# A prelude in a written order: the inverse's chain first, the first softmax in two halves of tokens

## The chip, the cores and the metric

The kernel runs on one core of a Trainium2 chip. The metric is the device time of one execution in microseconds (us); lower is better. TensorE does matrix products, VectorE, ScalarE and GpSimd work element by element, and SyncE issues the DMAs. In the profile they are PE (PEld for its weight loads), DVE, ACT, POOL and SP.

## The reference

Three stages follow one another: a Nystrom attention, a gated feed-forward layer and a soft mixture of experts. Cut to what matters (8 batches, 8 heads, 576 tokens, head size 64, 32 landmarks):

```python
q_lm, k_lm = means of q, k over 18 tokens each          # landmarks
A  = softmax(q @ k_lm.T / 8)                            # 576 x 32
Bm = softmax(q_lm @ k_lm.T / 8)                         # 32 x 32
C  = softmax(q_lm @ k.T / 8)                            # 32 x 576
Z  = Bm.T / (norm_1(Bm) * norm_inf(Bm) + 1e-6)
for _ in range(6): Z = 2 * Z - Z @ Bm @ Z               # inverse
x  = A @ Z @ C @ v                                      # attention
x  = (silu(x @ w_gate) * (x @ w_val)) @ w_out           # 512 -> 1536 -> 512
logits = x @ phi                                        # soft mixture of 8 experts
out = softmax(logits) @ experts(softmax(logits, tokens).T @ x)
```

All is float32. The feed-forward weights arrive as 64-bit floats (w_cat: gate and value of one slice of 128 columns side by side; w_out) and are converted on the chip.

## The kernel before

The 1536 feed-forward columns are cut into 12 slices (j), the 576 tokens into two halves of 288. A unit (b, j) computes both halves of slice j for batch b: `mm3` (line 885) takes six products each for pg and pv out of A's softmax, split into a high and a low part (EH, EL), and of g = Z C v times the weights, split in the same way (GH by line 728, GL by line 742). ScalarE applies silu to pg (u, line 302), VectorE multiplies u by pv (hT, line 914) and transposes hT (line 762). Batch b+1's attention runs in between, cut into steps that lists of numbers place in the slots of the units, four slots a unit.

Batch 0 has nothing before it, so a prelude does its attention: `first_attention`. Landmark sums over q and k (line 323), scores for A, B and C (lines 530 and 366), the softmax of B, from it the start value R of an inverse (line 468), five rounds that square R (line 457) and multiply T by it (lines 478 to 481), in between C's softmax, its transposes (line 397) and its product with v (line 407). Then VD (line 515), the small matrix WB (line 524), and g of unit 0. A's softmax of batch 0 comes from the generator `a_softmax` over all 576 tokens: maximum (line 683), subtraction on GpSimd (684), exponent, sum (675), reciprocal, product on GpSimd (687), transpose (681), EH on ScalarE (689), EL on GpSimd (690).

A weight tile is converted by one Prelu on ScalarE (line 166), shifts on VectorE (line 182) and an or on VectorE (line 183), the last two once per 512 columns. A w tile has 1024 columns, a w_out tile 512. w_out tiles are then transposed and multiplied by phi (lines 259 to 275).

What is written sets no order here: a scheduler orders each engine's instructions by its own estimates, within the dependencies. Each engine runs its queue in that order. `SCHED` holds the places: `w` and `o` say in which slot a conversion begins, where a negative number means the prelude, `p` places w_out's further steps, `loads` is the order of the first DMAs behind q, k and the constants, `side` a string of steps that are mixed into the prelude. w0, w1 and w_out's tile 0 belong to the prelude.

Of the kernel before, what the change touches and what calls it, by code (L numbers as in the profile page):

```python
# [8 lines left out]
F32 = mybir.dt.float32  # L9
F32R = mybir.dt.float32r  # L10
# [9 lines left out]
M = 32  # L20
# [33 lines left out]
def nystrom_softmoe_kernel(  # L54
# [15 lines left out]
    pe, act, dve, pool, sp = nc.tensor, nc.scalar, nc.vector, nc.gpsimd, nc.sync  # L70

# [37 lines left out]
    def big(tag, name):  # L109
        return bigp.tile([128, 2048], F32, tag=tag, name=name)  # L110
# [170 lines left out]
    for j in range(NJ):  # L281
        for kind in "wo":
# [8 lines left out]
    side_pre = [f for k in sorted(side_w) if k < 0 for f in side_w[k]]  # L291
# [60 lines left out]
    def first_attention(side):  # L352
        b = 0
        ks, qs, AN, CE = attention_tiles(b)
        NBUF = big("w5", "newton").rearrange("p (i q m) -> p i q m", q=2, m=128)
# [54 lines left out]
        for quad in range(2):  # L410
            for hp in (2 * quad, 2 * quad + 1):
                landmark("k", b, hp, ks)
                landmark("q", b, hp, qs)
            a_scores(quad)
# [11 lines left out]
        for half in range(2):  # L426
            a_nat(0, half)
# [14 lines left out]
        for q in range(2):
            blockdiag(q, nrm[:, q, 0, :], bdB)
        mn = psp.tile([128, 512], F32, tag="l", name="m_nx")
        pe.matmul(mn[:, 0:128], bmask, nrm.rearrange("p q a m -> p (q a m)"), start=True, stop=True)
        side("b")
        for half in range(2):
            a_nat(1, half)
        c_max(0)
        c_exp(0)  # L450
        side("c")
# [9 lines left out]
        ms = squares(bdB)  # L461
        nx = ap.tile([128, 2, 2], F32, tag="nx", name="nx")
# [21 lines left out]
        side("d")  # L484
        mv = psp.tile([128, 512], F32, tag="l", name="m_v")
        for k in range(1, 6):
            ms = squares(R)
            if k > 1:
                T = t_step(T, k - 1)
            R = NBUF[:, k]  # L490
            dve.tensor_copy(R[:, 0, :], ms[0][:, 0:128])
            act.copy(R[:, 1, :], ms[1][:, 0:128])
            if k == 1:
                c_max(1)
                c_exp(1)
# [200 lines left out]


    G_t = {}

    def paired(b, j):  # L700
        return 0 < b < nb - 1 and not (b == nb - 2 and j >= NJ - 2)

    def g_product(b, j, n):

        w = w_t[j // 2].rearrange("p (u h f) -> p u h f", u=2, h=4)
        gs = [psp.tile([128, 512], F32, tag="x", name="g", bufs=3) for r in range(2)]
        for u in range(n):
            assert j + u in w_done
        for hp in range(4):
            for r in range(2):  # L710
                pe.matmul(gs[r][32 * hp:32 * hp + 32, 0:256 * n].rearrange("p (u f) -> p u f", u=n),  # L711
                          WB[b % 2][64 * r:64 * r + 64, hp, :], w[64 * r:64 * r + 64, j % 2:j % 2 + n, hp, :],
                          start=True, stop=True)
        if n == 2:
            side_b = (6 * (b - 1) + j // 2) % 2 == 0
            e, tag = (ap, "b") if side_b else (mp, "")
            parts = [(e.tile([128, 512], F32R, tag="GH" + tag, name="GH", bufs=2),
                      e.tile([128, 512], F32R, tag="GL" + tag, name="GL", bufs=2), gs[r]) for r in range(2)]
        else:
            GH = mp.tile([128, 512], F32R, tag="GH", name="GH", bufs=2)  # L720
            GL = mp.tile([128, 512], F32R, tag="GL", name="GL", bufs=2)
            parts = [(GH[:, 256 * r:256 * r + 256], GL[:, 256 * r:256 * r + 256], gs[r][:, 0:256]) for r in range(2)]
        for r, (H_, L_, g) in enumerate(parts):
            for u in range(n):
                for sel in range(2):
                    c = slice(256 * u + 128 * sel, 256 * u + 128 * sel + 128)
                    G_t[b, j + u, r, sel] = (H_[:, c], L_[:, c])
            act.copy(H_, g)  # L728
            gl_todo.append((L_, g, H_))

    def g_unit(b, j):

        if not paired(b, j):
            g_product(b, j, 1)
        elif j % 2 == 0:
            g_product(b, j, 2)

    gl_todo = []

    def g_low():  # L740
        for GL, g, GH in gl_todo:
            dve.tensor_tensor(out=GL, in0=g, in1=GH, op=ALU.subtract)  # L742
        gl_todo.clear()
# [248 lines left out]
    wo = {}  # L992
# [45 lines left out]
    for b in range(nb):  # L1038
        for j in range(NJ):
# [242 lines left out]
```

## Time and profile before

| | us |
|---|---|
| median of 3 runs | 693.27 (693.15 to 694.85) |
| the profiled execution | 693.29 |
| its span in the trace | 691.5 |

The difference of 1.8 us lies around the span. Busy shares of the span: PE 93%, PEld 69%, DVE 70%, ACT 44%, POOL 10%. These shares are means; the first 122 us, prelude and batch 0, are read by stretches. Times of instructions are counted from the start of the span. The granted clock is a share of 2.4 GHz.

### The profile page before, as it was taken

To read this page: it belongs to the slowest core of one execution; us is meant where nothing else is said; L and a number is where in the kernel's file an instruction comes from. 1 tells how busy PE (TensorE), PEld (TensorE's weight loads), DVE (VectorE), ACT (ScalarE), POOL (GpSimd) and SP (SyncE) were. 2 spreads that over 40 slices of the span, in tenths; PEclk is the share of its full clock that TensorE was granted. 3 is DMA by queue.
4 is the path that set the end of the run, shared out by engine and by line. 5 is a ranking of instruction groups with operands and counts; after the bars stand their busy time and mean duration, and the time that the engine had idled before them with its cause. 6 is when DMAs were issued, how large, how long until landed. Compare 5 with 4: busy or idle time off the path is not lost.

```text
span 691.5 us, 18581 instructions
## 1 busy us (share of the span) xinstructions
PE 646.5 (93%) x7747; PEld 478.0 (69%) x7747; DVE 487.2 (70%) x1189; ACT 306.5 (44%) x775; POOL 72.2 (10%) x81
## 2 busy tenths in 40 slices
PE   5799999999999999999999999999999999999991
PEld 2566667766877787778776877687768876773561
DVE  5999989878667976797579757985786664540341
ACT  2567875356335533463345334533463352321441
POOL 0401012012001200120012001200120000010000
PEclk9899999999999999999999999999999999999997
DMA  8797873142204220322032302230212499599998
GB/s 294 243 361 275 300 263 116 65 138 70 70 2 136 70 72 2 116 78 84 2 101 82 96 1 89 79 110 2 82 50 63 149 301 283 186 295 319 348 371 309
DMA packets 59988, 105.03 MB, mean 152 GB/s; under 512 B 3968, under 2 KB 29696, under 8 KB 58368
## 3 DMA queue, kind: packets, MB, share of 16 engines
q1 hardware_dynamic: 59904, 103.84, 45.8%
q8 instruction: 61, 1.00, 0.6%
q14 instruction: 23, 0.19, 0.1%
HBM read 91.24 MB, written 12.58 MB: 150 GB/s over the span
## 4 chain that ended last, share of the span: by engine, by line
PE 68%; DVE 16%; ACT 7%; issue 3%; DMA 3%; POOL 1%; SPq 0%; ACTq 0%; POOLq 0%; DVEq 0%
PE pg L885 19%; PE pv L885 17%; PE g L711 6%; PE l L757 4%; PE m_n L638 3%; PE m_d L856 3%; PE m_f L1215 2%; PE m_f L1167 2%; DMA q<-in_qT_dram 2%; PE m_a L530 2%; DVE bd L312 2%; ACT L302 2%; DVE GL L742 1%; PE m_o L1198 1%; DVE qs L323 1%
## 5 line engine op out<-in xcount | busy, mean ns | idle before, releaser
L302 ACT ACTIVATE u<-pg 128x288 f32<-128x288 f32 x174 | 71.6, 412 | 148.7 <-PE pg L885 142.9
L914 DVE TENSOR_TENSOR hT<-u,pv 128x288 f32<-128x288 f32 x174 | 78.2, 450 | 56.2 <-PE pv L885 50.3
L885 PE MATMUL pg<-EH,GH 128*128 128x288 f32 x384 | 96.8, 329 | 2.6 <-ACT GH L728 1.6
L885 PE MATMUL pv<-EH,GH 128*128 128x288 f32 x384 | 91.4, 312 | 1.8 <-issue 1.6
L742 DVE TENSOR_TENSOR GL<-g,GH 128x512 fp32r<-128x512 f32 (+1 forms) x122 | 66.4, 569 | 32.6 <-ACT GH L728 32.3
L885 PE MATMUL pg<-EH,GL 128*128 128x288 f32 x384 | 86.0, 299 | 0.0
L885 PE MATMUL pg<-EL,GH 128*128 128x288 f32 x384 | 84.0, 298 | 0.0
L885 PE MATMUL pv<-EH,GL 128*128 128x288 f32 x384 | 83.1, 295 | 0.0
L885 PE MATMUL pv<-EL,GH 128*128 128x288 f32 x384 | 82.7, 296 | 0.0
L728 ACT CAST GH<-g 128x512 fp32r<-128x512 f32 (+1 forms) x122 | 54.3, 497 | 56.3 <-PE g L711 56.2
L885 PEld LDWEIGHTS pg<-EH,GH 128*128 128x128 f32 x384 | 59.9, 189 | 23.6 <-issue 18.9
L885 PEld LDWEIGHTS pv<-EH,GH 128*128 128x128 f32 x384 | 61.5, 188 | 19.6 <-issue 18.0
L762 DVE STREAM_TRANSPOSE HB<-hT 128x576 f32<-128x576 f32 x96 | 73.9, 770 | 1.3
L885 PEld LDWEIGHTS pg<-EH,GL 128*128 128x128 f32 x384 | 62.4, 188 | 2.2 <-issue 2.1
L885 PEld LDWEIGHTS pg<-EL,GH 128*128 128x128 f32 x384 | 61.7, 188 | 1.8 <-issue 1.8
L885 PEld LDWEIGHTS pv<-EH,GL 128*128 128x128 f32 x384 | 61.9, 188 | 0.5 <-issue 0.5
L885 PEld LDWEIGHTS pv<-EL,GH 128*128 128x128 f32 x384 | 61.6, 188 | 0.9 <-issue 0.9
L711 PE MATMUL g<-w,WB 64*32 64x512 f32 (+1 forms) x976 | 56.5, 510 | 0.4 <-ACT WB L524 0.4
L757 PE MATMUL l<-hT,P_sb 128*32 128x128 f32 (+1 forms) x768 | 47.4, 298 | 0.6 <-DVE hT L914 0.6
L757 PEld LDWEIGHTS l<-hT,P_sb 128*32 128x32 f32 x768 | 15.9, 108 | 40.0 <-issue 17.9
L856 PE MATMUL m_d<-HB,HB 32*32 32x384 f32 x1116 | 39.6, 491 | 0.3 <-DVE GL L742 0.3
L684 POOL TENSOR_TENSOR AN<-AN,mxA 128x576 f32<-128x576 f32 x16 | 18.4, 1169 | 181.1 <-DVE mxA L683 165.2
(238 smaller groups left out, 963.2 us busy)
## 6 DMA issues: line engine op xcount, KB each, us to landing
k<-in_kT_dram SPq DMA_DIRECT2D x52, 288.0 KB, 3.9
ffn<-in_w_dram SPq DMA_DIRECT2D x13, 1024.0 KB, 9.4
ffn<-in_w_dram SPq DMA_DIRECT2D x24, 512.0 KB, 8.8
HB<-in_w_cat_dram SPq DMA_DIRECT2D x8, 1024.0 KB, 7.5
v<-in_v_dram SPq DMA_DIRECT2D x8, 1024.0 KB, 5.7
q<-in_qT_dram SPq DMA_DIRECT2D x28, 288.0 KB, 3.2
HB<-in_w_out_dram SPq DMA_DIRECT2D x12, 512.0 KB, 4.9
wr<-in_w_cat_dram SPq DMA_DIRECT2D x4, 1024.0 KB, 8.5
```

What stands on the lines that cost most here:

```text
L302: i = act.activation(*a, **kw)
L312: dve.tensor_tensor(out=dst[:, q, :].rearrange("p (h m) -> p h m", h=4), in0=src.unsqueeze(1).to_broadcast([128, 4, 32]), in1=bm3, op=ALU. ...
L638: pe.matmul(m[:, 96 * q:96 * q + 96], bd[:, q, :], RV[:, q, :], start=True, stop=True)
L684: lambda q: pool.tensor_tensor(out=AN[q], in0=AN[q], in1=bc[q], op=ALU.subtract),
L711: pe.matmul(gs[r][32 * hp:32 * hp + 32, 0:256 * n].rearrange("p (u f) -> p u f", u=n), WB[b % 2][64 * r:64 * r + 64, hp, :], w[64 * r:64 * ...
L728: act.copy(H_, g)
L742: dve.tensor_tensor(out=GL, in0=g, in1=GH, op=ALU.subtract)
L757: pe.matmul(L[32 * c:32 * c + 32, 0:32 * k], P_sb[:, j, :], main[:, 0:k, c, :], start=j == 0, stop=j == NJ - 1)
L762: dve.transpose(HB[b % 2][:, S * j:S * j + S].rearrange("p (t r) -> p t r", r=32), hT[:, 0:S].rearrange("p (t r) -> p t r", r=32))
L856: pe.matmul(ms[a][32 * g:32 * g + 32, 0:384].rearrange("p (j f) -> p j f", j=NJ), d_of(a, g, k), hb[32 * a:32 * a + 32, :, 4 * k + g, :], ...
L885: pe.matmul(ps[:, 0:HALF], G_t[b, j, q, sel_][h], e[:, q, ts_], start=n == 0, stop=n == 5)
L914: dve.tensor_tensor(out=o, in0=u, in1=pv[:, 0:HALF], op=ALU.mult)
```

## The change

The prelude is written as one list, and `keep_order` ties each instruction of PE, ACT and DVE in it to the one before it on the same engine, so that the written order is the queue's order. What belongs to batch 0 is issued behind the last of them on its engine (`after_first`, until batch 1).

In the list the B scores come as soon as the landmarks are there, and B's softmax and the squares before the rest. A's softmax of batch 0 is done in two halves of 288 tokens: the first half between the rounds, the second behind VD, WB, EL of the first half and g of unit 0. Subtraction, product and EL of it are done by DVE, not POOL. Conversions of w0 and w1 stand in the list, w1's with the low words taken off by ACT (`lw`); w_out's tiles 0 and 1 go to slots 1 and 4. The loads come in the order w0, v0, w1, q and k of batch 1, phi, o0, w2, w3, o1, w4, v1.

```diff
 SCHED = {
-    'w': [[-22, 2], [-12, 2], [0, 3], [1, 3], ...
-    'o': [[-6, 1], [3, 2], [5, 3], ...
+    'w': [[0, 0], [0, 0], [0, 3], [2, 3], ...
+    'o': [[1, 2], [4, 2], [5, 3], ...
-    'loads': ['w1', 'q0', 'o0', 'w0', 'v0', 'o1', 'q1', 'v1', 'w2', 'w4', 'p', 'w3'],
+    'loads': ['w0', 'v0', 'w1', 'q0', 'q1', 'p', 'o0', 'w2', 'w3', 'o1', 'w4', 'v1'],
-    'lw': [0, 0, 0, ...
+    'lw': [0, 1, 0, ...
...
+    def keep_order(start):
+        last = {}
+        for i in nc.cur_bb.bb.instructions[start:]:
+            if i.engine in ENGINES:
+                if i.engine in last:
+                    tc.add_manual_dep(i, last[i.engine].name, mybir.DependencyInfo(
+                        mybir.DependencyClass.NoSync, mybir.DependencyReason.DATA), reason="keep_order")
+                last[i.engine] = i
+        return last.values()
...
+        def a_sub(q, h):
+            dve.tensor_tensor(out=AN[q][:, ts_[h], :], in0=AN[q][:, ts_[h], :], in1=bc(q, h), op=ALU.subtract)
+        def a_exp(q, h):
+            in_order("exp", AN[q][:, ts_[h], :], AN[q][:, ts_[h], :], AF.Exp, scale=SC / SEG)
+        def e_low(q, h):
+            dve.tensor_tensor(out=EL[:, q, cs_[h]], in0=AT[q][:, cs_[h]], in1=EH[:, q, cs_[h]], op=ALU.subtract)
...
             if k == 1:
+                both(a_sub, 0)
+                both(a_exp, 0)
+                c_max(0)
+            if k == 2:
+                c_exp(0)
                 c_max(1)
+                both(a_sum, 0)
+            if k == 3:
+                c_t(0)
                 c_exp(1)
+                a_inv(0)
+                both(a_mul, 0)
+            if k == 4:
                 c_t(1)
                 c_v(0, mv)
+                both(a_back, 0)
+            if k == 5:
                 c_v(1, mv)
+                both(e_high, 0)
+                w0[1]()
+                w0[2]()
...
         w_blocks(b, VD, T)
+        both(e_low, 0)
+        g_unit(0, 0)
+        both(a_max, 1)
+        g_low()
+        w1[0]()
+        both(a_sub, 1)
+        both(a_exp, 1)
+        both(a_sum, 1)
+        a_inv(1)
+        both(a_mul, 1)
+        both(a_back, 1)
+        both(e_high, 1)
+        both(e_low, 1)
+        for f in w1[1:]:
+            f()
...
+    start = len(nc.cur_bb.bb.instructions)
+    first_attention()
+    after_first = ctx.enter_context(ExitStack())
+    for i in keep_order(start):
+        after_first.enter_context(tc.issue_after(i))
     load_w(5)
-    for f in side_pre:
-        f()
-    g_unit(0, 0)
-    g_low()
```

VectorE's queue of the kernel before, from VD to the first hT of batch 0 (ks and qs are the landmarks of batch 1, HB_86 holds a w_out tile):

```order
L183 SCALAR_TENSOR_TENSOR HB_86<-HB_86 128x512
L515 TENSOR_SCALAR VD<-m_v_409,rc 128x64 x2
L323 TENSOR_REDUCE ks<-k_0_112 128x32
L323 TENSOR_REDUCE ks<-k_1_116 128x32
L323 TENSOR_REDUCE ks<-qk_124 128x32
L323 TENSOR_REDUCE ks<-qk_127 128x32
L323 TENSOR_REDUCE qs<-q_0_110 128x32
L742 TENSOR_TENSOR GL<-g,GH 128x256 x2
L323 TENSOR_REDUCE qs<-q_1_114 128x32
L323 TENSOR_REDUCE qs<-qk_124 128x32
L323 TENSOR_REDUCE qs<-qk_127 128x32
L914 TENSOR_TENSOR hT<-u,pv 128x288
```

The same queue of the changed kernel, the end of the second half's softmax up to the first hT and the next (w_235 is the tile of w0 and w1, w_462 that of w2 and w3):

```order
L498 STREAM_TRANSPOSE AT<-AN_143 128x288
L504 TENSOR_TENSOR EL<-AT,EH 128x288 x2
L190 SCALAR_TENSOR_TENSOR w_235<-w_235,HB_85 128x512 x2
L334 TENSOR_REDUCE ks<-k_0_116 128x32
L990 TENSOR_TENSOR hT<-u,pv 128x288
L334 TENSOR_REDUCE ks<-k_1_120 128x32
L193 TENSOR_SCALAR w_462<-w_462 128x512 x2
L194 SCALAR_TENSOR_TENSOR w_462<-HB_85,w_462 128x512
L193 TENSOR_SCALAR HB_86<-HB_86 128x512
L407 TENSOR_TENSOR GL<-g,GH 128x256 x2
L194 SCALAR_TENSOR_TENSOR HB_86<-HB_86 128x512
```

Eight landmarks and the w_out tiles stood ahead of the first hT; now one landmark does, and the others and the w_out tiles stand among the products of the first units, while a half of the softmax has come in ahead.

ScalarE's queue of the changed kernel, from the last T of the rounds to the first u (w_235 is again the tile of w0 and w1, HB_85 the raw words):

```order
L577 COPY newton<-m_T 128x256
L619 ACTIVATE RV<-m_v,stat 128x64 x2
L648 COPY WB_75<-m_w 128x128
L393 CAST GH<-g 128x256 x2
L177 ACTIVATE w_235<-HB_85 128x1024
L310 ACTIVATE AN_142<-AN_142 128x288
L310 ACTIVATE AN_143<-AN_143 128x288
L501 CAST EH<-AT 128x288 x2
L184 ACTIVATE HB_85<-HB_85 128x1024
L313 ACT_TABLE_LOAD
L313 ACTIVATE u<-pg 128x288
```

And before:

```order
L509 ACTIVATE RV<-m_v,stat 128x64 x2
L492 COPY newton<-m_n 128x128
L481 COPY newton<-m_T 128x256 x2
L524 COPY WB_75<-m_w 128x128
L728 CAST GH<-g 128x256 x2
L260 COPY HB_86<-m_wt 128x512
L302 ACT_TABLE_LOAD
L302 ACTIVATE u<-pg 128x288
```

RV (Cv in the code) has moved from ahead of the last two copies of T to behind the last, and between the first GH and the table load there now stand both parts of w1's conversion, two exponents and two copies to EH.

## Rows read from the trace of the kernel before

**Rows 1.** Windows: us, busy us of each engine, granted clock, DMA share, GB/s.

```profile
14.40:24.20 9.80, 3.26 (x12) 2.48 (x13) 9.36 (x33) 5.94 (x14) 3.39 (x3) 0.74 0.99 339
24.20:43.00 18.80, 16.37 (x206) 13.47 (x207) 17.64 (x37) 10.87 (x28) 5.20 (x5) 0.96 0.68 232
43.00:71.10 28.10, 25.71 (x290) 17.95 (x289) 25.89 (x60) 20.11 (x46) 2.49 (x2) 1.00 0.85 315
71.10:122.00 50.90, 49.55 (x567) 37.56 (x567) 46.35 (x111) 34.57 (x88) 6.24 (x5) 1.00 0.63 227
```

**Rows 2.** Timeline, VectorE, batch 0: start us, us, instruction, [idle before <-releaser].

```profile
42.53 0.44 DVE L914 TENSOR_TENSOR hT<-u,pv 128x288 f32<-128x288 f32 x1
45.44 0.72 DVE L182 TENSOR_SCALAR w<-w 128x512 int32<-128x512 int32 x2
46.08 1.29 DVE L183 SCALAR_TENSOR_TENSOR w<-HB,w 128x512 int32<-128x512 int32 x2
...
70.67 0.45 DVE L914 TENSOR_TENSOR hT<-u,pv 128x288 f32<-128x288 f32 x1 [0.57 <-ACT u L302]
...
121.52 0.46 DVE L914 TENSOR_TENSOR hT<-u,pv 128x288 f32<-128x288 f32 x1 [0.63 <-PE pv L885]
```

**Rows 3.** Timeline, VectorE, from the last landmark to R.

```profile
9.63 0.75 DVE L323 TENSOR_REDUCE ks<-qk 128x32 f32<-128x576 f32 x1
...
14.25 0.25 DVE L421 TENSOR_REDUCE stat<-m_a 128x1 f32<-128x32 f32 x2
...
17.57 1.81 DVE L437 TENSOR_SCALAR nrm<-nrm,stat 128x32 f32<-128x32 f32 x2
...
21.51 0.27 DVE L463 TENSOR_REDUCE nx<-m_nx 128x4 f32<-128x128 f32 x1
...
23.59 0.59 DVE L468 SCALAR_TENSOR_TENSOR newton<-m_n,rc,cst 128x128 f32<-128x128 f32 x2
```

**Rows 4.** Groups by shape, TensorE's scores, 4 to 11.5 and 12.5 to 14.4 us.

```profile
L530 PE MATMUL m_a<-q,ks 64*32 64x288 f32 x16 | 3.5, 684 | 0.9 <-DVE ks L323 0.9
...
L530 PE MATMUL m_a<-qk,ks 64*32 64x288 f32 x8 | 1.2, 405 | 0.0
```

**Rows 5.** Groups by shape, VectorE, prelude: xcount | busy us, mean ns | idle.

```profile
L183 DVE SCALAR_TENSOR_TENSOR w<-HB,w 128x512 int32<-128x512 int32 x4 | 3.8, 974 | 0.0
...
L183 DVE SCALAR_TENSOR_TENSOR w<-wr,w 128x512 int32<-128x512 int32 x4 | 2.7, 684 | 0.0
...
L437 DVE TENSOR_SCALAR nrm<-nrm,stat 128x32 f32<-128x32 f32 x2 | 1.8, 948 | 0.0
...
L312 DVE TENSOR_TENSOR bd<-nrm,cst 128x128 f32<-128x128 f32 x2 | 0.5, 274 | 0.0
...
L441 DVE TENSOR_SCALAR nrm<-cst,stat 128x32 f32<-128x32 f32 x2 | 0.4, 226 | 0.0
```

**Rows 6.** Groups, GpSimd, up to 43 us.

```profile
L684 POOL TENSOR_TENSOR AN<-AN,mxA 128x576 f32<-128x576 f32 x2 | 2.3, 1156 | 15.9 <-DVE stat L435 15.9
```

**Rows 7.** Timeline, TensorE, a product of the fifth round.

```profile
36.54 0.39 PE L479 MATMUL m_T<-newton 128*128 128x128 f32 x2
```

**Rows 8.** Timeline, ScalarE, from the last T to the first u.

```profile
37.46 0.37 ACT L481 COPY newton<-m_T 128x256 f32<-128x256 f32 x1 [1.30 <-PE m_T L479]
...
39.47 0.65 ACT L728 CAST GH<-g 128x256 fp32r<-128x256 f32 x2 [0.80 <-PE g L711]
...
40.62 1.28 ACT L302 ACT_TABLE_LOAD   x1
41.92 0.41 ACT L302 ACTIVATE u<-pg 128x288 f32<-128x288 f32 x1
```

**Rows 9.** Groups by shape, ScalarE, up to 60 us.

```profile
L166 ACT ACTIVATE w<-HB 128x1024 f32<-128x1024 f32 x5 | 5.7, 1146 | 0.0
```

**Rows 10.** TensorE behind its longest idle stretch: timeline, then a window.

```profile
19.73 0.77 PE L457 MATMUL m_n<-bd 128*128 128x128 f32 x2 [5.34 <-DVE stat L438]
...
19.50:25.50 6.00, 4.56 (x18) 3.78 (x19) 5.63 (x24) 3.49 (x8) 2.07 (x2) 0.50 1.00 329
```

More of the change, by code (lines that the diff above doesn't have):

```diff
@@ L281, in nystrom_softmoe_kernel @@
     for j in range(NJ):
-        for kind in "wo":
+        for kind in "wo"[j < 2:]:
             first, span = S_[kind][j]
@@ L290, in nystrom_softmoe_kernel @@
         side_w[p0 + p1 + p2].append(lambda j=j: p_sum(j))
[L291 removed]
+    assert min(side_w) >= 0
     fence = {}
@@ L350, in attention_tiles, with paired, g_product, g_unit @@
         return ks, qs, AN, CE
-    def first_attention(side):
+    G_t = {}
+    def paired(b, j):
+        return 0 < b < nb - 1 and not (b == nb - 2 and j >= NJ - 2)
+    def g_product(b, j, n):
+        w = w_t[j // 2].rearrange("p (u h f) -> p u h f", u=2, h=4)
+        gs = [psp.tile([128, 512], F32, tag="x", name="g", bufs=3) for r in range(2)]
+        for u in range(n):
+            assert j + u in w_done
+        for hp in range(4):
+            for r in range(2):
+                pe.matmul(gs[r][32 * hp:32 * hp + 32, 0:256 * n].rearrange("p (u f) -> p u f", u=n),
+                          WB[b % 2][64 * r:64 * r + 64, hp, :], w[64 * r:64 * r + 64, j % 2:j % 2 + n, hp, :],
+                          start=True, stop=True)
+        if n == 2:
+            side_b = (6 * (b - 1) + j // 2) % 2 == 0
+            e, tag = (ap, "b") if side_b else (mp, "")
+            parts = [(e.tile([128, 512], F32R, tag="GH" + tag, name="GH", bufs=2),
+                      e.tile([128, 512], F32R, tag="GL" + tag, name="GL", bufs=2), gs[r]) for r in range(2)]
+        else:
+            GH = mp.tile([128, 512], F32R, tag="GH", name="GH", bufs=2)
+            GL = mp.tile([128, 512], F32R, tag="GL", name="GL", bufs=2)
+            parts = [(GH[:, 256 * r:256 * r + 256], GL[:, 256 * r:256 * r + 256], gs[r][:, 0:256]) for r in range(2)]
+        for r, (H_, L_, g) in enumerate(parts):
+            for u in range(n):
+                for sel in range(2):
+                    c = slice(256 * u + 128 * sel, 256 * u + 128 * sel + 128)
+                    G_t[b, j + u, r, sel] = (H_[:, c], L_[:, c])
+            act.copy(H_, g)
+            gl_todo.append((L_, g, H_))
+    def g_unit(b, j):
+        if not paired(b, j):
+            g_product(b, j, 1)
+        elif j % 2 == 0:
+            g_product(b, j, 2)
+    gl_todo = []
+    def g_low():
+        for GL, g, GH in gl_todo:
+            dve.tensor_tensor(out=GL, in0=g, in1=GH, op=ALU.subtract)
+        gl_todo.clear()
+    def first_attention():
         b = 0
         ks, qs, AN, CE = attention_tiles(b)
+        mxA = A_t[b][1]
+        EH, EL = E_t[b]
         NBUF = big("w5", "newton").rearrange("p (i q m) -> p i q m", q=2, m=128)
@@ L408, in c_v, with bc, a_max, a_sum @@
                               v_t[b][0:k, c, 128 * h + 64 * q:128 * h + 64 * q + 64], start=c == 0, stop=c == 4)
[L410 to L414, printed above, removed]
+        AT = [ap.tile([128, S], F32, tag="AT", name="AT", bufs=2) for q in range(2)]
+        ts_ = [slice(9 * half, 9 * half + 9) for half in range(2)]
+        cs_ = [slice(HALF * half, HALF * half + HALF) for half in range(2)]
+        def bc(q, h):
+            return mxA[:, q, ts_[h]].unsqueeze(2).to_broadcast([128, 9, M])
+        def a_max(q, h):
+            dve.tensor_reduce(mxA[:, q, ts_[h]], AN[q][:, ts_[h], :], axis=AX.X, op=ALU.max)
+        def a_sub(q, h):
+            dve.tensor_tensor(out=AN[q][:, ts_[h], :], in0=AN[q][:, ts_[h], :], in1=bc(q, h), op=ALU.subtract)
+        def a_exp(q, h):
+            in_order("exp", AN[q][:, ts_[h], :], AN[q][:, ts_[h], :], AF.Exp, scale=SC / SEG)
+        def a_sum(q, h):
+            dve.tensor_reduce(mxA[:, q, ts_[h]], AN[q][:, ts_[h], :], axis=AX.X, op=ALU.add)
+        def a_inv(h):
+            dve.tensor_scalar(mxA[:, :, ts_[h]], mxA[:, :, ts_[h]], 1e-9, None, ALU.add)
+            dve.reciprocal(mxA[:, :, ts_[h]], mxA[:, :, ts_[h]])
+        def a_mul(q, h):
+            dve.tensor_tensor(out=AN[q][:, ts_[h], :], in0=AN[q][:, ts_[h], :], in1=bc(q, h), op=ALU.mult)
+        def a_back(q, h):
+            dve.transpose(AT[q][:, cs_[h]].rearrange("p (t r) -> p t r", r=32), AN[q][:, ts_[h], :])
+        def e_high(q, h):
+            act.copy(EH[:, q, cs_[h]], AT[q][:, cs_[h]])
+        def e_low(q, h):
+            dve.tensor_tensor(out=EL[:, q, cs_[h]], in0=AT[q][:, cs_[h]], in1=EH[:, q, cs_[h]], op=ALU.subtract)
+        def both(f, h):
+            for q in range(2):
+                f(q, h)
+        w0 = conversion("w", 0)
+        w1 = conversion("w", 1)
+        for hp in range(4):
+            landmark("q", b, hp, qs)
+            landmark("k", b, hp, ks)
+            if hp == 1:
+                a_scores(0)
         b_scores()
+        a_scores(1)
         cm = c_scores(0)
@@ L425, in first_attention @@
                            accum_out=stat[:, q, 5:6])
-        for half in range(2):
-            a_nat(0, half)
+        for r in range(2):
+            a_nat(r, 0)
         for r in range(2):
@@ L437, in first_attention @@
             dve.tensor_scalar(nrm[:, q, 0, :], nrm[:, q, 0, :], stat[:, q, 7:8], None, ALU.mult)
-        dve.tensor_reduce(stat[:, :, 0:1], nrm[:, :, 0, :], axis=AX.X, op=ALU.add)
         bdB = ap.tile([128, 2, 128], F32, tag="bd", name="bd", bufs=2)
         for q in range(2):
+            blockdiag(q, nrm[:, q, 0, :], bdB)
+        dve.tensor_reduce(stat[:, :, 0:1], nrm[:, :, 0, :], axis=AX.X, op=ALU.add)
+        for q in range(2):
             dve.tensor_scalar(nrm[:, q, 1, :], i4, stat[:, q, 0:1], None, ALU.mult)
[L442 to L451, printed above, removed]
         def squares(src):
@@ L461, in first_attention @@
         ms = squares(bdB)
+        mn = psp.tile([128, 512], F32, tag="l", name="m_nx")
+        pe.matmul(mn[:, 0:128], bmask, nrm.rearrange("p q a m -> p (q a m)"), start=True, stop=True)
+        for r in range(2):
+            c_copy(r, 1, cm[r])
+        w0[0]()
+        for r in range(2):
+            a_nat(r, 1)
         nx = ap.tile([128, 2, 2], F32, tag="nx", name="nx")
@@ L482, in t_step @@
             return Tn
-        side("d")
+        both(a_max, 0)
         mv = psp.tile([128, 512], F32, tag="l", name="m_v")
@@ L487, in first_attention @@
             ms = squares(R)
-            if k > 1:
-                T = t_step(T, k - 1)
+            old = R
             R = NBUF[:, k]
@@ L695, in a_softmax @@
             seq.add(("asm", b))
[L698 to L743, printed above, removed]
     L_t = {}
```

38 lines of the change are left out of this document (12 added, 26 removed), and 9 rows, old and new, of the table SCHED.

## The prediction

> **What bounds the kernel now.** I read the page first. Its chain of waits names TensorE for most of the span and VectorE second, an average over unlike stages, so I cut the span into stretches [rows 1]. There the reader is to see two things. From 14.4 us on VectorE never rests: 9.36 of 9.8 us up to the start value of the inverse, 17.64 of 18.8 to the first product, 25.89 of 28.1 from there to 71.1 us. And TensorE is as full as VectorE from 43 to 71.1 us (25.71 of 28.1) and fuller from 71.1 to 122 (49.55 of 50.9). So the edited stretch, up to 43 us, belongs to VectorE, the next 28 us to both, and what follows to TensorE: a delay that survives until 71 us is kept, and a lead too.
>
> I use three marks, all VectorE's products hT of batch 0: the first ends at 42.97 us, the eighth (second half of unit 3) at 71.12, the twenty-third at 121.98 [rows 2]. Sums are made against the profiled execution, 693.29 us with a span of 691.5; the median shown is 693.27, so no correction is needed.
>
> **The inverse starts earlier.** The landmarks end at 10.38 us in both, set by their DMAs [rows 3]. Before, the B scores come late on TensorE, and VectorE takes their maximum at 14.25; the start value R (L468) is done at 24.18. Between stand maxima and sums of the A softmax, maxima over C, and L437, 1.81 us for two instructions [rows 3]. After, B follows the landmarks at once: 10.4 + some 0.6 gives 11.0, first maximum 11.4. The four passes of A and C scores behind it are 0.96 each at the pace of the 0.68-us records [rows 4] (eight tiles share a pass), plus 0.65 for one copy of C: 15.6. Squares and norm product 0.85, then 1.4 for norms and R on VectorE (0.27 and 0.59 in [rows 3], three short ones between): R at 17.8, 6.4 us earlier.
>
> L437's 948 ns against 226 for the same shape at L441, and the second steps of w's conversion (974 against 684), have GpSimd tensor operations beside them [rows 5, 6]. With GpSimd out of the prelude but for one instruction these stalls go: 2 x 0.72 + 4 x 0.29 = 2.6 us of VectorE. The Trainium skill, "SBUF — State Buffer", section "Who interferes with whom", says that VectorE and GpSimd share a pair of ports, and that the second to start is blocked for the other's whole instruction. The trace agrees (948 against 226), and by that rule the sum would gain these 2.6 us; but the same operations now cost VectorE its own time.
>
> That time: subtract, multiply and low part, twelve instructions of 128x288. The trace has no such instruction from SBUF alone. The nearest is the product hT, 0.44 us, some 0.37 from start to start; from below the 128x128 product at 0.27 [rows 5], spaced 0.20, from above half of GpSimd's 1.16 for twice the columns [rows 6]. I take 0.37: 4.4 us (2.4 to 7.0). Halving adds 0.4 (eight reductions at 0.36 for four at 0.66, four transposes at 0.39 for two at 0.69), and w1's low words by ScalarE take off two shifts, 0.7. VectorE's total is thus up by 4.1 and down by 2.6. But what decides is where it waits and what is put off.
>
> **The five rounds.** TensorE's 128x128 records in them are 70, two of which end 0.39 after they start together at 0.28 each [rows 7], so 0.11 apart: 7.7 us at full clock, and C times v comes on top. Before, from R to the last T took 24.18 to 37.83, 13.65 us [rows 3, 8], with conversions in VectorE's queue. After, going through the written order instruction by instruction with these durations, C's copies and exponents hold TensorE for some 2 us, and C times v takes 1.6: 11.4 (7.7 to 13.65). Last T at 29.2.
>
> **The end of the prelude.** Before, Cv, its product and VD lay under the fifth round, and from the last T to the first copy of g it is 1.64 us (37.83 to 39.47) [rows 8]. The written order has Cv behind T's copy: 0.51 + 0.6 + 0.46 more, of which 0.5 was due anyway. I get 3.8 us: g's copy at 33.0. The lead of 8.6 us at the last T is 6.5 here.
>
> **The second half of the softmax.** Before, EH and EL are whole when g is; now units of the second half of tokens wait for a chain that VectorE starts in earnest behind GL. On the path: g's two copies 0.65, GL 0.71, two subtractions 0.74, exponent 0.46, two sums 0.70, reciprocal 0.40, two products 0.74, two transposes 0.92, copies to EH 0.84 (ScalarE). Then w1's low words 1.0, the table load 1.28 and u 0.41 on ScalarE [rows 8, 9], all behind EH in its queue; hT behind one landmark on VectorE 0.75. Sum 9.6 us: first hT ends at 42.6, 0.4 before the old 42.97. VectorE has stood idle for about 8 us in between (squares, VD, GL, EL), since nothing else is in its queue. TensorE waits from about 36 to 39.3 for EH, and w1 is ready only at 41.6, so unit 1 starts at 43.6.
>
> **What was put off.** The order shows the price. Before, all eight landmarks of batch 1 and both of the first w_out tiles stand ahead of the first hT. After, one landmark does; seven and both conversions stand between the first and eighth hT. Landmarks: 7 x 0.67 = 4.7; conversions 2 x (0.34 + 0.61) = 1.9, from pairs in the timeline, which start 0.07 closer than one of them lasts [rows 2, 3]. Together 6.6 us more on an engine that had 28.1 - 25.9 = 2.2 us of idle there. So the eighth hT ends at 42.6 + 25.9 + 6.6 = 75.1 with no idle time and at 77.3 with the old: middle 76.2, 5.1 late. From there to the twenty-third both orders have the same instructions on VectorE. TensorE was full but for 50.9 - 49.55 = 1.35 us. I let all of that be won back: 3.8 late, and blocks 1 to 7 keep it. 693.3 + 3.8 = 697.1 us.
>
> **Loads.** The new order issues w2, w3 and w4 before anything that waits late for TensorE; before, w2 goes out behind v of batch 1, which waits for C times v. Earlier weights are worth little: their conversions stand behind the second half of the softmax now, and before, VectorE's idle 2.2 us up to the eighth hT hold all that it waited for them. v and w0 are issued ninth to eleventh, and the queue moves 339 GB/s [rows 1], so they land before they are used.
>
> **Unknown sizes.** The records before 11.5 us take 0.68 us and those from 12.5 on 0.41 [rows 4]. If the quick pace is there by 12, all is 0.9 earlier; if the slow one lasts to 24, 3.7 later. The twelve instructions move the first hT by -1.0 to +1.3 (six are on its path). Both ends: -1.9 to +5.0 around 3.8.
>
> **Rivals.**
> One, the lead is kept, faster. TensorE, not VectorE, sets block 0: the landmarks of batch 1 are needed only for its WB, late in batch 0, so they could cost nothing, and the 2.39 us that TensorE idled up to 71 us go as well, since weights land earlier. Then -0.4 - 2.4, about 690.5. For it: TensorE is 91% busy there. Against: the landmarks stand between hTs in one queue, and two hT tiles hold the products back.
> Two, the clock falls in the hole. Before, after TensorE's 5.34 us of idleness, the granted clock was 0.50, 1.2 GHz, from 19.5 to 25.5 us [rows 10]. The hole from 36 to 39.3 is shorter. If it does the same, 6 us of TensorE's work at half pace cost up to 3 us: 700. The Trainium skill, "TensorE: Matmul & The Clock Gate", section "Why this matters for your kernels", warns against idle gaps between bursts of matmuls for this reason. By that rule the change makes a new gap where before there was none; the trace shows a fall after 5.34 us of idleness and says nothing of 3.3.
> Three, the delay is nearly absorbed: the quick pace early (-0.9), no idle at all up to the eighth hT (-1.1), the cheap end of the twelve (-1.0), together 694.1, no change to be told. For it speaks that VectorE's total work hardly grows; against, that three ends must come together.
>
> **How the numbers follow.** Changes of under 0.3%, 2.1 us, can't be told from none. Forecast with its own range 695 to 699.5: 0.50. Rival two and the slow pace, above 699.5: 0.14. Rival three, 691.2 to 695.4: 0.16. Rival one, below 691.2: 0.20. Hence slower 0.64, same 0.16, faster 0.20. The range leaves out half of rival one and of the slow tail: 691 to 701.
>
> **What would show it.** R done near 17.8; last T near 29; first copy of g near 33; TensorE idle for 3 us or more between the first and second half of unit 0; first hT near 42.6; eighth hT near 76; blocks 1 to 6 as long as before. I am wrong if the eighth hT ends before 72, or if block 0 ends early although it doesn't.

## The result and the profile after

| | before | after |
|---|---|---|
| median of 11 runs each, us | 693.92 (692.58 to 696.42) | 696.83 (696.03 to 704.5) |
| ratio after / before | | 1.0059, 95% interval 1.0037 to 1.0082 |
| the profiled execution, us | 693.29 | 696.34 |
| its span, us | 691.5 | 694.6 |

Slower by some 0.6%, where 697.1 (691 to 701) was forecast. In the kernel after, L990 is hT, L334 a landmark, L524 B's maximum, L567 R, L586 VectorE's copy of a square, L577 T's copy on ScalarE, L393 the copy of g, L501 EH.

VectorE of the kernel after, timeline, against [rows 2, 3]:

```profile
10.32 0.75 DVE L334 TENSOR_REDUCE ks<-qk 128x32 f32<-128x576 f32 x1
12.44 0.29 DVE L524 TENSOR_REDUCE stat<-m_a 128x1 f32<-128x32 f32 x2 [1.37 <-PE m_a L654]
...
17.75 0.61 DVE L567 SCALAR_TENSOR_TENSOR newton<-m_n,rc,cst 128x128 f32<-128x128 f32 x2
...
28.03 0.29 DVE L586 COPY newton<-m_n 128x128 f32<-128x128 f32 x1 [2.24 <-PE m_n L549]
...
32.46 0.48 DVE L625 TENSOR_SCALAR VD<-m_v,rc 128x64 f32<-128x64 f32 x2 [2.00 <-PE m_v L622]
...
42.97 0.44 DVE L990 TENSOR_TENSOR hT<-u,pv 128x288 f32<-128x288 f32 x1
...
74.74 0.81 DVE L990 TENSOR_TENSOR hT<-u,pv 128x288 f32<-128x288 f32 x2
...
124.79 0.45 DVE L990 TENSOR_TENSOR hT<-u,pv 128x288 f32<-128x288 f32 x1 [0.63 <-PE pv L961]
```

The reader is to see that R is done at 18.36 us, 5.8 us earlier than before, and the first hT ends at 43.41, 0.4 us later: between the two VectorE waits 2.24 us for the fifth square and 2.00 us for VD's product. The eighth hT (first of the pair at 74.74) ends at 75.19, 4.1 us late, the twenty-third at 125.24, 3.3 late, and the span is 3.1 us longer.

ScalarE after, timeline, against [rows 8], and TensorE's longest wait:

```profile
31.12 0.37 ACT L577 COPY newton<-m_T 128x256 f32<-128x256 f32 x1 [0.88 <-PE m_T L575]
...
34.53 0.65 ACT L393 CAST GH<-g 128x256 fp32r<-128x256 f32 x2 [0.81 <-PE g L376]
...
39.19 0.79 ACT L501 CAST EH<-AT 128x288 fp32r<-128x288 f32 x2 [2.29 <-DVE AT L498]
39.89 1.18 ACT L184 ACTIVATE HB<-HB 128x1024 int32<-128x1024 uint16 x1
41.08 1.28 ACT L313 ACT_TABLE_LOAD   x1
42.38 0.41 ACT L313 ACTIVATE u<-pg 128x288 f32<-128x288 f32 x1
...
39.67 0.61 PE L961 MATMUL pg<-EH,GH 128*128 128x288 f32 x1 [2.86 <-ACT EH L501]
```

The last T comes 6.3 us earlier than before (ends at 31.49, not 37.83) and g's copy 4.9 earlier, and then all hangs on EH of the second half: TensorE waits 2.86 us for it. Windows of the kernel after, against [rows 1, 10] and in their columns; the last two lie inside the others:

```profile
18.40:31.50 13.10, 11.96 (x150) 10.71 (x149) 9.06 (x27) 7.35 (x23) 0.72 (x1) 0.87 1.04 396
31.50:43.40 11.90, 7.54 (x64) 5.84 (x64) 9.38 (x25) 7.23 (x14) 0.00 (x0) 0.86 0.92 324
43.40:75.20 31.80, 27.23 (x302) 18.09 (x294) 30.83 (x73) 22.36 (x51) 1.01 (x1) 1.00 0.76 260
75.20:125.20 50.00, 49.57 (x564) 37.29 (x557) 46.34 (x110) 34.15 (x86) 7.59 (x7) 1.00 0.54 186
20.00:22.00 2.00, 2.00 (x11) 2.00 (x11) 1.93 (x7) 0.75 (x3) 0.00 (x0) 0.50 1.06 393
40.00:42.00 2.00, 2.00 (x9) 2.00 (x9) 1.38 (x4) 1.98 (x2) 0.00 (x0) 0.50 0.88 302
```

VectorE works 9.06 of 13.1 us in the rounds and 9.38 of 11.9 up to the first hT, where before it worked 17.64 of 18.8. Then it is full, 30.83 of 31.8. And the granted clock is 0.50, that is 1.2 GHz, in two places, the second right behind the hole.

VectorE's groups of the kernel after up to 46 us, against [rows 5]:

```profile
L194 DVE SCALAR_TENSOR_TENSOR w<-HB,w 128x512 int32<-128x512 int32 x3 | 2.0, 681 | 0.0
...
L482 DVE TENSOR_TENSOR AN<-AN,mxA 128x288 f32<-128x288 f32 x4 | 1.6, 451 | 0.0
...
L537 DVE TENSOR_SCALAR nrm<-nrm,stat 128x32 f32<-128x32 f32 x2 | 0.4, 238 | 0.0
```

The stretched instructions are gone (948 to 238 ns, 974 to 681; the 684 ns group of [rows 5] lies at 49 to 60 us, behind the prelude), and the subtractions cost 451 ns each, a pair 0.82 us.

### The profile page after: what moved, and what is told of

Read it like the earlier page. It is cut to its first block, busy times and chain, and to the rows that moved or that the text cites. A ratio compares the mean times of both kernels' runs of the same rounds, so it can differ in the third digit from the quotient of the medians.

```text
span 694.6 us, 18587 instructions
## 1 busy us (share of the span) xinstructions
PE 648.9 (93%) x7747; PEld 479.9 (69%) x7747; DVE 488.2 (70%) x1205; ACT 308.3 (44%) x780; POOL 64.3 (9%) x75
## 4 chain that ended last, share of the span: by engine, by line
PE 74%; DVE 13%; ACT 6%; issue 2%; DMA 2%; POOL 1%; SPq 0%; DVEq 0%; ACTq 0%; POOLq 0%
PE pg L961 20%; PE pv L961 18%; PE g L376 6%; PE l L833 5%; PE m_d L932 4%; PE m_n L762 3%; PE m_f L1281 2%; PE m_f L1233 2%; DVE qs L334 1%; PE m_a L654 1%; PE m_c L654 1%; PE m_o L1264 1%; ACT L313 1%; DMA q<-in_qT_dram 1%; DVE GL L407 1%
## 5 line engine op out<-in xcount | busy, mean ns | idle before, releaser
L990 DVE TENSOR_TENSOR hT<-u,pv 128x288 f32<-128x288 f32 x174 | 78.2, 451 | 54.0 <-PE pv L961 48.5
L393 ACT CAST GH<-g 128x512 fp32r<-128x512 f32 (+1 forms) x122 | 54.4, 496 | 58.2 <-PE g L376 58.2
L808 POOL TENSOR_TENSOR AN<-AN,mxA 128x576 f32<-128x576 f32 x14 | 15.9, 1158 | 189.6 <-DVE mxA L807 134.6
```

Source lines behind the costliest of these rows:

```text
L808: lambda q: pool.tensor_tensor(out=AN[q], in0=AN[q], in1=bc[q], op=ALU.subtract),
L990: dve.tensor_tensor(out=o, in0=u, in1=pv[:, 0:HALF], op=ALU.mult)
```

## The experiments

Theory: VectorE stands idle in the written order, with work put off that could have been done there, and what it is late by, TensorE keeps. Rivals: the clock that falls at TensorE's hole (its wait of 2.86 us between the two halves of unit 0); the loads; VectorE doing GpSimd's work; the written order as such. The runs lie on three chips, each with the kernel before beside it, and the ratios are to that one. "Busy" is VectorE's busy time in the 25 us from 18.4 to 43.4 us; hTs are ends in the profiled execution; the clock is the mean granted clock over the timed runs (for the kernel before, over those beside the experiments).

| kernel | ratio to before (95%) | clock | busy | hT 1, 8, 23 |
|---|---|---|---|---|
| before | 1 | 0.981 | 23.84 | 43.0, 71.1, 122.0 |
| after | 1.0059 (1.0037 to 1.0082) | 0.980 | 18.44 | 43.4, 75.2, 125.2 |
| e0_after | 1.0069 (1.0042 to 1.0097) | 0.976 | 18.10 | 43.6, 75.4, 125.4 |
| e1_landmarks | 1.0031 (1.0010 to 1.0051) | 0.979 | 22.81 | 42.5, 70.8, 121.0 |
| e2_free | 1.0013 (0.9992 to 1.0035) | 0.982 | 22.07 | 39.2, 68.2, 120.3 |
| e4_pool | 1.0055 (1.0034 to 1.0075) | 0.978 | 14.27 | 42.3, 72.6, 122.1 |
| e5_second_half | 0.9993 (0.9976 to 1.0011) | 0.985 | 21.13 | 40.5, 70.8, 120.9 |
| e6_warm | 1.0074 (1.0045 to 1.0102) | 0.984 | 19.43 | 42.5, 73.5, 123.6 |
| e7_loads (one run) | | 0.970 | 17.75 | 44.3, 78.7, 128.7 |
| e8_combo | 0.9994 (0.9975 to 1.0012) | 0.983 | 22.31 | 41.0, 71.7, 120.9 |
| e9_lm_warm | 1.0028 (1.0007 to 1.0050) | 0.987 | 21.71 | 43.8, 72.1, 122.1 |
| e10_combo_warm | 0.9982 (0.9959 to 1.0006) | 0.985 | 22.87 | 41.1, 71.9, 121.1 |
| e11_free | 1.0003 (0.9990 to 1.0016) | 0.980 | 22.08 | 40.1, 70.4, 122.4 |
| e12_look (one run) | | 0.985 | 18.21 | 44.1, 75.9, 125.9 |

From the twenty-third hT to the end of the span it takes 569.5 us before and 569.4 after, and 568.0 to 571.3 in the other profiled executions: the change's 3 us arise in the first 122 us, and a single execution can differ by 1 to 2 us behind them.

e0_after is the changed kernel once more, on the chip of e6_warm, e7_loads and e8_combo. I expected it 3 us (1.5 to 4.5) above the kernel before; its median was 4.8 above (698.66 against 693.86).

**e1_landmarks.**

```diff
+            lm([0, 0, 0, 0, 3][k - 1])  # landmarks of batch 1
             dve.tensor_copy(R[:, 0, :], ms[0][:, 0:128])
...
+        lm(3)                           # before VD
+        lm(2)                           # before g_low
```

> The changed kernel, with the eight landmarks of batch 1 written into the list where VectorE stood idle: three ahead of the copy of the fifth square (idle 2.24 us there), three ahead of VD (2.00 us), two ahead of GL. Theory (VectorE idles in the written order and the work put off to the units is the price): first hT within 0.6 us of the 43.41 us of the changed kernel, the eighth some 4.7 us earlier than 75.20, at 70 to 71.5, and 692.5 us in all (691.5 to 694). Rival, loads: the landmarks wait in the list for q and k of batch 1, the prelude gets 1 to 2 us longer, 697 to 698. Rival, the halved softmax itself (its extra work and TensorE's hole) is the price and the landmarks were hidden: eighth hT at 74.5 to 75.5, 696 to 697.

VectorE of this kernel, timeline; L334 is a landmark, L601 the copy of a square, L641 VD, L1008 hT:

```profile
24.66 0.71 DVE L334 TENSOR_REDUCE ks<-k 128x32 f32<-128x576 f32 x1
25.30 0.74 DVE L334 TENSOR_REDUCE qs<-q 128x32 f32<-128x576 f32 x1
25.95 0.74 DVE L334 TENSOR_REDUCE ks<-k 128x32 f32<-128x576 f32 x1
26.61 0.28 DVE L601 COPY newton<-m_n 128x128 f32<-128x128 f32 x1
...
30.27 0.74 DVE L334 TENSOR_REDUCE qs<-qk 128x32 f32<-128x576 f32 x1
31.02 0.48 DVE L641 TENSOR_SCALAR VD<-m_v,rc 128x64 f32<-128x64 f32 x2
...
70.36 0.45 DVE L1008 TENSOR_TENSOR hT<-u,pv 128x288 f32<-128x288 f32 x1
```

The waits of 2.24 and 2.00 us are filled, the copy and VD have no bracket any more, and the eighth hT ends at 70.81, 4.4 us earlier, inside the theory's 70 to 71.5. From the first hT to the eighth it takes 28.3 us, as before (28.2) and not 31.8 as in the changed kernel: the landmarks were what made that stretch longer. The first hT, at 42.49, came 0.3 earlier than expected, with rounds of 11.96 us. The time did not follow in full: 1.0031 where 692.5 us had been expected, some 0.3% less than the changed kernel, with intervals that overlap; e9_lm_warm below repeats it (1.0028). So the landmarks were part of the price, not all of it. This profiled execution was the fastest of its eleven (691.9 to 698.39), so its marks flatter it.

**e5_second_half.**

```diff
+            if k == 5:
+                both(a_max, 1)
+                both(a_sub, 1)
             dve.tensor_copy(R[:, 0, :], ms[0][:, 0:128])
...
                 both(e_high, 0)
+                both(a_exp, 1)
...
+        both(a_sum, 1)
+        a_inv(1)
+        both(a_mul, 1)                  # before VD
...
+        both(a_back, 1)
         g_low()
+        both(e_high, 1)
         w1[0]()
```

> The changed kernel, with the second half of the softmax drawn ahead: its maxima and subtractions in front of the copy of the fifth square, exponents behind EH of the first half, sums, reciprocal and products in front of VD, transposes in front of GL, EH in front of w1's conversion. Theory (the same as above): TensorE's hole of 2.86 us between the halves of unit 0 shrinks to under 0.8, first hT 40.2 to 41.5, eighth 72 to 73.5, total 694 us (693 to 695.5). Rival, clock: the granted clock of 0.50 from 40 to 42 us goes with the hole and gives 1.5 us more: eighth at 71, total 692.5. Rival, the put-off landmarks alone decide: the eighth hT stays at 74.5 to 75.5, 696 to 697.

TensorE of this kernel where the hole was, and ScalarE ahead of the eighth hT, timelines:

```profile
36.35 0.42 PE L962 MATMUL pv<-EL,GH 128*128 128x288 f32 x2
36.61 0.43 PE L962 MATMUL pv<-EH,GL 128*128 128x288 f32 x2
36.87 0.43 PE L962 MATMUL pg<-EH,GH 128*128 128x288 f32 x2
...
68.63 1.28 ACT L313 ACT_TABLE_LOAD   x1
69.92 0.41 ACT L313 ACTIVATE u<-pg 128x288 f32<-128x288 f32 x1
```

The products of the second half follow those of the first without a gap. The first hT came at 40.49, 2.9 us earlier than in the changed kernel, and the loss is gone: 0.9993, the interval apart from the changed kernel's. The landmarks are as late as in the changed kernel, so the rival that they alone decide is refuted too. The eighth hT came at 70.83, earlier than the theory's 72 to 73.5 and where e1_landmarks has it: in both, u waits there for the table load at 68.6 behind the exponents of batch 1's softmax. The eighth hT and the median (692.96) are those of the clock rival (71 and 692.5), so this run does not decide against it; e6_warm and e9_lm_warm do.

**e2_free.**

```diff
-    for i in keep_order(start):
-        after_first.enter_context(tc.issue_after(i))
```

> The changed kernel without the ties of the written order, so that the scheduler places the same instructions: by its order R comes behind 13 more instructions of VectorE, and the second half of the softmax, two landmarks and a w_out conversion move ahead of the first hT. Theory: VectorE idles under 4 us up to 43 us instead of about 8, R is done near 22 us instead of 18.4, and the lead that was wasted is replaced by work done: 694.5 us (693 to 696.5). Rival, the written order is a gain and the halving with VectorE in place of GpSimd is the whole loss: 697 to 700.

R came at 20.52, VectorE idled 2.9 of 25 us, the ratio is 1.0013. The theory's numbers held: with the same instructions and a later inverse the scheduler lost less than the list that put the inverse first (up to 1.0035, where the changed kernel begins at 1.0037).

**e4_pool.** `dve.tensor_tensor` became `pool.tensor_tensor` in `a_sub`, `a_mul` and `e_low`.

> The changed kernel, with the twelve 128x288 subtractions, products and low parts given back to GpSimd. Theory: VectorE has 12 x 0.41 = 4.9 us less work but idles anyway; the second half's chain, six of them, gets longer, at about 0.58 to 0.65 us each on GpSimd instead of 0.41, and their neighbours on VectorE stretch: first hT 44 to 45.5, eighth 75.5 to 77, total 697.3 us (696.5 to 698.5). Rival, VectorE's own work is the price of the change: eighth hT 4 us earlier, 692.5 to 694.

GpSimd's groups of this kernel, then two lines of its timeline:

```profile
L504 POOL TENSOR_TENSOR EL<-AT,EH 128x288 fp32r<-128x288 f32 x4 | 3.4, 881 | 5.3 <-ACT EH L501 5.3
L482 POOL TENSOR_TENSOR AN<-AN,mxA 128x288 f32<-128x288 f32 x4 | 2.6, 672 | 1.5 <-DVE mxA L479 1.5
...
18.48 1.30 POOL L482 TENSOR_TENSOR AN<-AN,mxA 128x288 f32<-128x288 f32 x2
18.50 0.74 DVE L444 TENSOR_REDUCE stat<-CE 128x1 f32<-128x576 f32 x1
```

VectorE is 4 us less busy and the time is that of the changed kernel (1.0055), with a longer chain: from the last T to the first hT 12.7 us instead of 11.9. So VectorE's work in itself is not the price. The marks missed my expectation, the first hT 1.7 us early; this execution was the fastest of six, its landmarks were done at 10.58 and its rounds took 11.96 us, so I read nothing from its later marks. GpSimd's work did not stretch the reduction that ran beside it (0.74 us, as in the changed kernel).

**e6_warm.**

```diff
+        for _ in range(4):
+            pe.matmul(mn[:, 128:288], ident, cst[:, 128:288], start=True, stop=True)
...
+            if (b, j, half) == (0, 0, 0):
+                with tc.issue_after(pv_last):
+                    keep_warm(10)
```

> The changed kernel with idle stretches of TensorE filled by products whose result nobody reads: four of 128x160 behind the norm product, ten behind the first half of unit 0 (both where TensorE idled, 1.34 and 2.86 us). Nothing else is touched. Theory (VectorE's put-off work): the granted clock is 1.00 up to 48 us, the rounds from R to the last T take 12.0 us instead of 13.1, so the marks up to the first hT come 0.5 to 1.2 us earlier, the eighth hT as much and no more; total 0.5 to 1.2 us below the changed kernel run beside it. Rival, clock: what the hole costs is mostly the clock, which falls for a varying time from one execution to the next: the mean granted clock rises from about 0.980 to 0.986 or more, the scatter of the times shrinks to that of the kernel before, and the total falls by 2.5 us or more.

TensorE of this kernel in the place of the hole, timeline (a float32 product leaves two records, so 20 are the ten products), and a window:

```profile
35.75 2.88 PE L848 MATMUL warm<-cst 128*128 128x160 f32 x20
38.77 0.40 PE L963 MATMUL pg<-EH,GH 128*128 128x288 f32 x1
```

```profile
36.00:44.00 8.00, 6.54 (x54) 5.19 (x53) 7.17 (x18) 5.69 (x10) 0.00 (x0) 1.00 0.70 229
```

The clock stayed at 1.00, and the eighth hT came 1.9 us earlier than in e0_after beside it: 1.1 of that came before the first hT, with rounds of 12.0 us instead of 13.5, and only 0.7 behind it. But the times did not fall (1.0074 against 1.0069) and their scatter did not shrink (694.75 to 705.11). So the clock behind the hole is not most of what the change costs; a difference under 2 us could not be seen here.

**e7_loads and e12_look.** In the first `q0` stands second in `loads`; the second is the changed kernel again.

> The changed kernel with q and k of batch 1 (first half) issued ahead of v and w1, so that only w0 is queued right behind the loads of batch 0. Theory of the loads (v and w1 share the queue with the last q and k of batch 0, and that is why the landmarks end 0.7 us later than before): landmarks done at 10.4 us, R at 17.7. Rival (it varies from one execution to the next, whatever the order): 10.6 to 11.1 us.

> One more execution of the changed kernel, profiled. Theory of the hole's clock: the granted clock falls again behind the hole at 36.8 to 39.7 us, for a length that lies anywhere between the 3.4 us seen twice and the 18 us of e7_loads, and the eighth hT lies between 75.2 and 78.7 accordingly. Rival: the fall is always 3.4 us with this order and the long one belongs to the other order of loads: 75.2 to 75.4.

e7_loads had its landmarks done at 11.20 us, later than with v and w1 ahead, so the theory of the loads fails in this one execution. They ended anywhere from 10.40 to 11.08 in the other runs of the written list. Its windows, the first of them ahead of its hole (39.1 to 40.6 us):

```profile
31.00:33.00 2.00, 0.89 (x7) 0.56 (x6) 0.36 (x2) 0.79 (x3) 0.00 (x0) 1.00 1.05 414
34.00:48.00 14.00, 11.30 (x67) 8.91 (x68) 11.75 (x29) 10.21 (x19) 0.00 (x0) 0.50 0.93 344
```

e12_look's 40 to 44:

```profile
40.00:44.00 4.00, 3.60 (x28) 3.08 (x28) 3.25 (x7) 3.97 (x6) 0.00 (x0) 0.59 0.37 131
```

and e1_landmarks's 33 to 43:

```profile
33.00:43.00 10.00, 7.71 (x52) 6.03 (x40) 8.08 (x19) 7.07 (x11) 0.00 (x0) 0.52 0.89 321
```

The clock is 0.50 for 14 us and more in e7_loads, and its eighth hT comes at 78.67; for some 3 us in e12_look, as in after and e0_after (75.9, 75.2, 75.4). The rival, 3.4 us with this order, fits three executions of it (e12_look's eighth hT is later because R was, at 18.87). But the long fall is not one behind the hole, as I had taken it to be: it begins at 33 us, behind TensorE's short waits for RV and VD (0.73 and 0.38 us), some 6 us ahead of the hole. e1_landmarks has one from the same place, from 32 to 43 us, and its eighth hT is yet 4.4 us earlier than the changed kernel's. What sets the length of a fall stays open.

**e8_combo, e9_lm_warm, e10_combo_warm, e11_free.** e8_combo is e5_second_half with three landmarks as well, e10_combo_warm that with five unread products behind the norm product; e9_lm_warm is e1_landmarks with the ten products of e6_warm in the hole; e11_free is e5_second_half without the ties.

```diff
                 both(a_sub, 1)
+                lm(1)
...
         both(e_low, 1)
+        lm(2)
```

and the products of e10_combo_warm:

```diff
+        wm = psp.tile([128, 512], F32, tag="x", name="warm", bufs=3)
+        for _ in range(5):
+            pe.matmul(wm[:, 0:160], ident, cst[:, 128:288], start=True, stop=True)
         for r in range(2):
             c_copy(r, 1, cm[r])
```

> The second half of the softmax drawn ahead as in the run e5_second_half, and three landmarks of batch 1 put where VectorE still idled there: one ahead of the copy of the fifth square (0.82 us), two ahead of the last step of w1 (1.52 us). Theory: VectorE's idle time up to the first hT falls from 3.3 to about 1.2 us, first hT 40.3 to 41, eighth 1.3 to 2.0 us earlier than 70.82, at 68.8 to 69.6; total 691.5 us (690 to 693), 1 us or so below the kernel before. Rival: from 70.8 on TensorE sets the pace, since the eighth hT stood at 70.82 in two runs with different edits: eighth at 70.5 to 71, total as in e5_second_half, 692 to 694.

> The eight landmarks of batch 1 in VectorE's idle time, as in the run e1_landmarks, and besides TensorE's hole between the halves of unit 0 filled by ten products of 128x160 whose result nobody reads. Open is why e1_landmarks, whose eighth and twenty-third hT came as early as those of e5_second_half (70.8 and 120.9 to 121.0), took 0.3% more than the kernel before and e5_second_half did not. Theory of the hole's clock (the first has the hole, the second not, and behind a hole the granted clock stays low for a time that differs between executions): mean granted clock 0.983 or more instead of 0.979, ratio to the kernel before 0.998 to 1.001. Rival (the difference is chance or lies elsewhere): clock 0.979, ratio 1.002 to 1.005, as without the products.

> e8_combo with five such products behind the norm product, in a PSUM tile of their own, while TensorE waits 1.34 us for R. Theory (a half-pace stretch behind that wait costs the rounds 1.2 to 1.5 us, the rest is pinned later): R at 17.9 as before, R to the last T 12.0 us instead of 13.5, first hT 39.5 to 40, eighth 69.5 to 71 since batch 1's exponents hold ScalarE there; ratio to the kernel before 0.997 to 1.000. Rival (what TensorE gains in the prelude goes through to the end): 1.5 us less, ratio 0.9965 or lower.

> e5_second_half without the ties of the written order: the same list, but the scheduler places it. Theory (what counts is what VectorE does while it would wait, and scheduler and list are equally good at that once the second half is drawn ahead): R later (20 to 22 us), first hT 39 to 40.5, eighth 68 to 70.5, ratio to the kernel before 0.998 to 1.001. Rival (the chain of the inverse in its written order is worth its lead): eighth 72 or later, ratio 1.002 or more.

In e8_combo the first hT came at 41.0, the eighth at 71.73, later than theory and rival had it, and the ratio stayed at 0.9994, the rival's time. Its seventh hT was 1.1 us earlier than e5_second_half's (63.70 against 64.84), its eighth 0.9 later. What holds it is in its window 64 to 71 us, VectorE and ScalarE both full, TensorE not:

```profile
64.00:71.00 7.00, 5.12 (x41) 4.10 (x40) 7.00 (x15) 6.96 (x19) 1.57 (x1) 1.00 0.58 207
```

So the rival named the place rightly and the engine wrongly. In e9_lm_warm the mean clock rose from 0.979 to 0.987 and the ratio did not (1.0028 against 1.0031): the clock's theory falls a second time. From the first hT to the eighth it takes 28.3 us again. Its marks, 72.1 and 122.1 us, are 1.3 and 1.1 later than e1_landmarks', since its rounds took 13.95 us and not 11.96; that is 0.2% of the 0.4% between e1_landmarks and e5_second_half, and the rest lies within the intervals. In e10_combo_warm R came late (18.87, where 17.9 was expected), R to the last T took 12.42 us, the first and eighth hT came 1 us later than expected, and the ratio of 0.9982 is the lowest here: below the changed kernel's beyond doubt, not below before's (up to 1.0006). e11_free, R at 21.62, is as fast as its tied twin (1.0003): theory right.

## Why the prediction was right

The forecast came true by the mechanism that it named: the inverse's lead is lost on the chain of the second half, and work put off to the first units makes TensorE late. The terms were off by up to 1.7 us each, in both directions, and that their errors left 697.1 against 696.83 is luck.

- *Landmarks at 10.38 in both*: wrong by 0.7 in this execution (11.07); it varies. From there to R 7.3 us, predicted 7.4. The twelve instructions cost 0.37 us from start to start, as priced (a pair 0.82 us, one 0.45). L437's stall went as said, 948 to 238 ns, which agrees with the rule on shared ports in the Trainium skill ("SBUF — State Buffer", "Who interferes with whom").
- *The rounds, 11.4 us*: 13.13 measured. In three runs whose records were at the quick pace in them (e1_landmarks, e4_pool, e6_warm) they took 11.96 to 11.98. So the term was 0.6 too small, and the slow pace, which I had as an end of the range, costs 1.2 more.
- *Last T to g's copy, 3.8*: 3.04 (31.49 to 34.53). The sum was wrong: its terms, 1.64 + 0.51 + 0.6 + 0.46 - 0.5, make 2.7 and not 3.8. So the terms were 0.3 too small, and the slip made them 0.8 too large.
- *The second half*: hole 2.86 us where I said 3.3; g's copy to first hT 8.9 where I summed 9.6. First hT 43.41 for 42.6.
- *What was put off, 6.6 us*: the mis-sized term. VectorE did 30.83 us of work to the eighth hT instead of 25.89, so 4.9. The landmarks cost what I said, some 4.6; the two conversions some 1.2 more instead of 1.9, since before's second steps on HB were themselves stretched (897 ns on average, 670 after), and the instructions ran closer together. Eighth hT 75.2, in my 75.1 to 77.3.
- *Won back 1.35 by TensorE, 3.8 kept*: 0.8 won back, 3.1 kept in the span; blocks 1 to 7 as long as before (569.4 us against 569.5).
- *The reason*: each term could be taken out by itself. With the landmarks drawn into VectorE's idle time (e1_landmarks, e9_lm_warm) the stretch from the first hT to the eighth falls from 31.8 to 28.3 us, as before. With the second half drawn ahead (e5_second_half) the first hT comes 2.9 us earlier, and nothing is lost although the landmarks stay put off. I had named VectorE's idle time before the first hT (6.6 of the 25 us in the table, 1.2 before) and TensorE's hole, but not said that the idle time could hold either, nor that in the whole time the second half is worth more than the landmarks (some 0.7% against 0.3%).
- *Rival two, the clock*: it fell as that rival said, to 0.50 behind the hole (3.4 us, not 6). The Trainium skill, "TensorE: Matmul & The Clock Gate", section "Why this matters for your kernels", warns of such gaps; on the fall the trace agrees (0.50 from 39.6 to 43.0 us, behind 2.86 us without a product). But without that fall the time was the same twice (e6_warm, e9_lm_warm), within 2 us. Rivals one and three did not happen.

What stays open: the last 0.2% between e1_landmarks and e5_second_half, and what makes some executions of the changed kernel so long. They go with a low clock: the four of its eleven runs above 699 us (699.51 to 704.5) have the four lowest mean clocks (0.966 to 0.976), the other seven lie at 696.0 to 697.2 with 0.980 to 0.988. But the two longest of e6_warm (702.8 and 705.11) have its two lowest as well (0.979 and 0.977), with the hole filled, so it is not the hole alone; and the seven short ones are still 2 to 3 us above the median before.

## What to carry to other kernels

In this kernel the chain that came first was worth only what stood in the queues while it was waited for. When writing an order by hand, go through each engine's waits and try in them the start of the next long chain first, and independent work second. And look at where the next engine blocks: e8_combo's lead of 1.1 us over e5_second_half was gone at the exponents of the next batch, where ScalarE and VectorE were full.

## What the runs showed of the hardware

TensorE's pace in the first 23 us differs from one execution to the next, and the column of the granted clock does not always show it. TensorE of e12_look, timeline and window:

```profile
15.68 1.22 PE L549 MATMUL m_n<-bd 128*128 128x128 f32 x4
...
20.24 1.23 PE L549 MATMUL m_n<-newton 128*128 128x128 f32 x4 [0.35 <-ACT newton L587]
```

```profile
14.00:22.50 8.50, 6.33 (x36) 4.77 (x35) 7.25 (x29) 3.77 (x9) 0.73 (x1) 1.00 1.04 367
```

and of the kernel after, the same two groups:

```profile
15.88 0.71 PE L549 MATMUL m_n<-bd 128*128 128x128 f32 x4
...
19.43 1.19 PE L549 MATMUL m_n<-newton 128*128 128x128 f32 x4 [0.52 <-DVE newton L586]
```

Two such products, four records, take 1.22 us at the slow pace and 0.71 at the quick one, and in e12_look the column reads 1.00 while they are slow. In the kernel after the pace was quick at 15.88 and slow again at 19.43, where the column shows it (0.50). The rounds take 13.1 to 13.5 us in four executions of the changed list (after, e0_after, e7_loads, e12_look) and 11.96 to 13.95 in its variants, so marks of one profiled execution are good to 1 or 2 us here, no better.
